# A transformer block on one core: which side work runs beside the attention, and when its banks come back

## The chip, the core and the metric

The kernel runs on one core of a Trainium2 chip. The metric is device time in microseconds (us) of one execution. Five engines work side by side: TensorE (PE in the profile) multiplies matrices into the eight banks of PSUM, VectorE (DVE) and ScalarE (ACT) read those banks, GpSimd (POOL) works in SBUF, and SyncE (SP) issues the DMAs. Each takes its own instructions in order and waits for the others by semaphores.

## The reference

One block over 2048 rows of 512 numbers, with 32 heads of width 16 that share one key and one value head, and a bilinear gated feed-forward of inner width 1792. Six vectors from a condition `c` scale, shift and gate:

```python
sa, ca, ga, sb, cb, gb = (mod[:, 0], ..., mod[:, 5])          # mod = silu(c) @ w_mod
h = _layernorm(x) * (1 + ca) + sa
q = (h @ wq) per head; k = h @ wk; v = h @ wv                  # one k and one v for all heads
o = softmax(q k^T * Dh ** -0.5) v
x = x + ga * (o @ wo)
h = _layernorm(x) * (1 + cb) + sb
x = x + gb * (((h @ w_gate) * (h @ w_up)) @ w_down)
```

## The kernel before, in words

The rows are cut into 4 blocks of 512 (numbered 0 to 3), a block into 8 units of 4 heads, a unit into 32 steps: 16 tiles of 128 keys, two heads in each step. The main loop runs over 32 units and so over 1024 steps. A step issues two score matmuls (`sc`, L549) and their exponentials on ScalarE (`P`, L551), and two matmuls (`mx`, L507) with reductions on VectorE (`mpart`, L509) that find the row maxima of a step 40 steps ahead, so that the last 40 steps of the loop have none of these. Every odd step also issues the value matmuls (`pv`, L558) of the key tile before.

All else is **side work** of an earlier block, and runs in even steps, at most six pairs of half-array matmuls at a time (`BURST`): for block b its output projection (`wo_work`, L640), its second layer norm (`ln2_work`: four sets of transposes, L683, evicted by ScalarE into `hf`, L690, and split by GpSimd into two halves in 16 bits), and its feed-forward (gate and up, then `glu`, then down, L746). `duo` runs two groups of equal length at once on the two halves of the array (L440); one group takes the PSUM bank `misc`, the other the bank `spare`. One matmul of a full group becomes one pair. Groups have 12 matmuls, those of the down projection 42. A down projection has four groups, so two duos of 84 pairs.

Three score tiles in turn use the two banks `sc` and the bank `spare`, as long as no side work is under way and `spare["held"]` is zero; otherwise they alternate between the two. When a duo ends, its first group is evicted at once. The second is evicted two ticks later (a tick is a step), and in the same call the bank is given back to the scores:

```python
        def late():
            spare["held"] -= 1
            g1.post(ps[1])
```

The queue `fill` holds the side work with a gate (the step from which it may begin) and a due step. `pace` spreads what is left over the steps up to each due step, and leaves `RESERVE` ns of it, at `PAIR` ns a pair, for after the loop. At step 16 of a block's first unit the loop appends the work of the block before: output projection, the four sets of transposes ("solo"; each takes a turn of its own in an even step, 8 steps after the output projection and then every 2), and after 2 more steps the feed-forward. From the output projection's end to the feed-forward there is thus no side work. A new duo isn't begun in the last 16 steps (`LAST_TILES`).

After the loop stands the **tail**: what is left of block 2's feed-forward and all of block 3's, as full matmuls (`plain`, L465). `cover` puts numbers of them beside the last unit's softmax sums (stored, loaded as 128 rows, inverted, stored, loaded again: L579, L582, L585, L587, L591) and beside the norm.

Rows of 512 numbers of the residual stream (`x1`) live in a ring of 4 buffers from the output projection to the end of the down projection.

## Time and profile before

| | |
|---|---|
| time, median of 3 runs | 1826.44 us (1825.76 to 1830.4) |
| the profiled execution | 1827.18 us, its span 1825.4 us |
| granted TensorE clock, mean over the span | 0.989 |
| busy: TensorE, VectorE, ScalarE, GpSimd | 94%, 79%, 67%, 27% of the span |
| first exponential of the main loop, last one's end | 103.0 us, 1659.0 us |
| the tail, to the end of the span | 166 us |

A row of a timeline gives start and length in us, engine, line, operation, what it writes and reads, the count of instructions merged into it and, in brackets, how long the engine had been idle and what released it. A row of a table by windows gives the stretch, its length, the busy time and count of PE, PEld, DVE, ACT and POOL, the granted clock (1.00 is full), the DMA's share and GB/s. A matmul's busy time counts its latency too, so that busy shares of TensorE overstate its load.

### The profile page before, as it was taken

How to read it: one execution, taken by the hardware profiler on the slowest of the kernel's cores; microseconds unless marked ns; L12 is line 12 of the kernel's file. 1: busy time of each engine (PE TensorE's matmuls, PEld its weight loads, DVE VectorE, ACT ScalarE, POOL GpSimd, SP SyncE). 2: the span in 40 equal slices, each digit the busy share in tenths (PEclk: the TensorE clock that was granted, in tenths of full speed). 3: DMA queues.
4: the chain of work that ended last, by engine and by line, in shares of the span. 5: the costliest groups of instructions: out<-in, count | busy, mean ns of one | idle time of the engine just before them, and what ended most of it. 6: DMA issues, size and time to landing. Idle time of an engine off the chain costs nothing.

```text
span 1825.4 us, 32237 instructions
## 1 busy us (share of the span) xinstructions
PE 1714.7 (94%) x12643; PEld 554.1 (30%) x12643; DVE 1438.3 (79%) x2441; ACT 1217.3 (67%) x2269; POOL 488.7 (27%) x688
## 2 busy tenths in 40 slices
PE   6899999889989999999999999999989999998999
PEld 3332222222223333333223333333223323322444
DVE  7877999999998888888998888888989888911210
ACT  4567788777777767776677767676777777772110
POOL 5834453436566811010021010100011010111130
PEclk9999999999999999999999999999999999998999
DMA  5212222112221200000100000000100000001000
GB/s 189 91 69 94 60 69 61 49 44 65 82 70 55 55 15 9 5 14 17 50 9 15 9 15 9 6 14 20 46 8 15 9 15 9 11 4 39 18 1 23
DMA packets 49795, 66.58 MB, mean 36 GB/s; under 512 B 16166, under 2 KB 30314, under 8 KB 49644
## 3 DMA queue, kind: packets, MB, share of 16 engines
q1 hardware_dynamic: 48060, 64.33, 11.4%
q8 instruction: 99, 1.62, 0.4%
q14 instruction: 52, 0.43, 0.1%
q10 hardware_dynamic: 1584, 0.20, 0.1%
HBM read 51.12 MB, written 8.92 MB: 33 GB/s over the span
## 4 chain that ended last, share of the span: by engine, by line
PE 68%; DVE 17%; ACT 10%; issue 2%; DMA 2%; POOL 1%; SPq 0%; DVEq 0%; POOLq 0%; ACTq 0%
PE pv L558 22%; PE misc L440 17%; DVE mpart L509 13%; PE mx L507 10%; PE sc L549 10%; PE misc L465 8%; ACT P L551 8%; DVE gf L731 1%; DMA xbig<-in_A_x_dram 1%; ACT ev L564 1%; DVE x L640 0%; DVE x L746 0%; ACT qf L476 0%; DVE oc L591 0%; ACT q L475 0%
## 5 line engine op out<-in xcount | busy, mean ns | idle before, releaser
L509 DVE TENSOR_REDUCE mpart<-mx 128x1 f32<-128x512 f32 x2048 | 1294.2, 684 | 172.3 <-PE sc L549 136.3
L551 ACT ACTIVATE P<-sc 128x512 f32<-128x512 f32 x2048 | 1097.7, 599 | 391.6 <-PE sc L549 385.0
L549 PE MATMUL sc<-sst,kst 50*128 50x512 f16 x2048 | 630.5, 382 | 52.7 <-ACT P L551 35.3
L507 PE MATMUL mx<-kst,sst 48*128 48x512 f16 x2048 | 656.3, 383 | 22.8 <-DVE mpart L509 19.6
L558 PE MATMUL pv<-P,vst 128*32 128x512 f32 x4096 | 552.2, 612 | 0.0
L507 PEld LDWEIGHTS <-sst 48*128 48x128 f16 x2048 | 161.8, 94 | 602.7 <-issue 545.7
L732 POOL TENSOR_SCALAR glu<-gf 128x512 f16<-128x512 f32 x56 | 34.6, 618 | 556.0 <-DVE gf L731 555.9
L549 PEld LDWEIGHTS <-kst 50*128 50x128 f16 x2048 | 136.5, 94 | 107.0 <-issue 66.8
L440 PE MATMUL misc<-h2T,wg 64*128 64x512 f16 x1008 | 134.6, 375 | 7.7 <-DVE gf L731 7.7
L558 PEld LDWEIGHTS pv<-P,vst 128*32 128x32 f32 x4096 | 81.1, 108 | 186.4 <-issue 181.7
L440 PE MATMUL misc<-h2T,wu 64*128 64x512 f16 x1008 | 132.6, 375 | 0.4 <-ACT g L725 0.4
L731 DVE TENSOR_TENSOR gf<-misc,g 128x512 f32<-128x512 f32 x56 | 38.3, 686 | 102.4 <-PE misc L465 62.9
L594 POOL TENSOR_SCALAR och<-oc 128x512 f16<-128x512 f32 x15 | 9.3, 618 | 305.4 <-DVE oc L591 165.9
L440 PE MATMUL misc<-wd,glu 64*128 64x512 f16 x672 | 85.6, 375 | 1.9 <-DVE x L746 1.1
L725 ACT ACTIVATE g<-misc 128x512 f32<-128x512 f32 x56 | 34.0, 608 | 78.7 <-PE misc L465 75.5
L465 PE MATMUL misc<-wd,glu 128*128 128x512 f16 x336 | 74.0, 382 | 0.0
L440 PEld LDWEIGHTS <-wg 64*128 64x128 f16 x1008 | 50.7, 94 | 71.8 <-issue 19.4
L440 PEld LDWEIGHTS <-wu 64*128 64x128 f16 x1008 | 50.3, 94 | 60.2 <-issue 8.8
L733 POOL TENSOR_TENSOR glu<-gf,glu 128x512 f16<-128x512 f32 x56 | 64.7, 1155 | 4.7
L440 PE MATMUL misc<-h,wq 64*128 64x512 f16 x384 | 52.9, 391 | 1.6 <-ACT qf L476 1.6
L815 POOL TENSOR_TENSOR wsl<-wsl 128x448 f32<-128x448 f32 (+1 forms) x40 | 39.0, 975 | 55.9 <-DMA wsl<-in_B_w_up_dram 30.3
L817 POOL TENSOR_TENSOR kwb<-kwb,wsl 128x448 f32<-128x448 f32 (+1 forms) x40 | 47.6, 1189 | 3.1
(214 smaller groups left out, 912.8 us busy)
## 6 DMA issues: line engine op xcount, KB each, us to landing
wsl<-in_B_w_gate_dram SPq DMA_DIRECT2D x32, 224.0 KB
wsl<-in_B_w_up_dram SPq DMA_DIRECT2D x32, 224.0 KB
wsl<-in_B_w_down_dram SPq DMA_DIRECT2D x28, 256.0 KB
sst<-qd SPq DMA_DIRECT2D x186, 32.0 KB
qd<-q SPq DMA_DIRECT2D x16, 256.0 KB
oc<-ev SPq DMA_DIRECT2D x128, 32.0 KB
rr<-ri SPq DMA_DIRECT2D x16, 256.0 KB
xl<-in_A_x_dram SPq DMA_DIRECT2D x16, 256.0 KB
```

The source lines that it names most:

```text
L440: nc.tensor.matmul(p, left[64 * r:64 * r + 64], right[64 * r:64 * r + 64], start=start, stop=stop)
L465: nc.tensor.matmul(p, left, right, start=i == 0, stop=i == g.n - 1)
L507: nc.tensor.matmul(m, s[64 * a:64 * a + 48, p, t * 128:(t + 1) * 128], kst[64 * a:64 * a + 48, kc * 512:(kc + 1) * 512], start=True, stop= ...
L509: nc.vector.tensor_reduce(mparts[u][:, a, p, t, kc:kc + 1], m, axis=AX.X, op=OP.max)
L549: nc.tensor.matmul(t, kst[64 * a:64 * a + 50, kt * 128:(kt + 1) * 128], s[64 * a:64 * a + 50, p, :], start=True, stop=True)
L551: nc.scalar.activation(ptl[u, kt, p][:, a, :], t, AF.Exp)
L558: nc.tensor.matmul(pvb[u][32 * j:32 * j + 32, :], vst[:, kt, :], ptl[u, kt, p][:, a, :], start=(kt == 0), stop=(kt == KT - 1))
L731: nc.vector.tensor_tensor(gf, p, st["g", f], op=OP.mult)
L732: nc.gpsimd.tensor_scalar(st["glu"][:, 0, f, :], gf, 1.0, 0.0, op0=OP.mult, op1=OP.add)
L733: nc.gpsimd.tensor_tensor(st["glu"][:, 1, f, :], gf, st["glu"][:, 0, f, :], op=OP.subtract)
L815: nc.gpsimd.tensor_tensor(acc if i == 0 else t, t, t, op=OP.mult)
L817: nc.gpsimd.tensor_tensor(acc, acc, t, op=OP.add)
```

## The change

Six things, in one planner:

- The second duo of a block's down projection (blocks 0 and 1) is taken out of the block's own list (`carry`) and queued behind the next block's output projection, so that it runs during that block's second norm. Block 2 keeps both its duos.
- The sets of transposes leave the queue: they stand in a list `solos` with steps of their own, run in odd steps behind the value matmuls, and write one of the three `mx` banks instead of `misc` (in the tail, for block 3, still `misc`). The last entry of the list opens the gate of the feed-forward.
- In `duo` the bank is given back to the scores three ticks after the second eviction was issued, not with it.
- A duo may begin late in the loop if its first half fits (for the down projection 16 steps before the end); what isn't done when the loop ends runs as pairs ahead of the tail, and `cover` counts it.
- Output projection and carried duo are due 64 steps after they were queued (`SOON`), the rest of the feed-forward 16 instead of 12 steps into the next block (`DUE`), in the last block 4 instead of 8 steps before the end; the reserve for the tail is 31000 ns instead of 35000.
- The ring of `x1` has 6 buffers instead of 4.

```diff
-RESERVE = 35000.0
+RESERVE = 31000.0
-DUE = 12
+DUE = 16
+SOON = 64
 QDUE = 40
-LAST_TILES = 8
+LAST_DUE = -4
...
         def late():
+            g1.post(ps[1])
+            after(3, free)
+
+        def free():
             spare["held"] -= 1
-            g1.post(ps[1])
...
-                    x1 = work.tile([128, D], F32, name="x1", tag="x1", bufs=4)
+                    x1 = work.tile([128, D], F32, name="x1", tag="x1", bufs=6)
...
-                st["p"] = ps_misc()
+                st["p"] = ps_misc() if b == NB - 1 else ps_mx()
...
-            n += 4.0 if kind == "solo" else 2 * what[0].n
+            n += 0.0 if kind == "call" else 2 * what[0].n
...
     def open_gate(step):
         if not fill:
             return False
+        if fill[0][1] == "duo" and NU * NSTEP - step < 2 * -(-fill[0][2][0].n // BURST) + 2:
+            return False
...
-            if kind == "solo":
-                _, f, post = what
-                credit[0] -= 4.0
-                f()
-                if post:
-                    posts.append(post)
-                return
-            if NU * NSTEP - step < 2 * LAST_TILES:
-                fill.appendleft(([0, 0], kind, what, due))
-                return
+            if kind == "call":
+                what(step)
+                if not open_gate(step):
+                    return
+                _, kind, what, due = fill.popleft()
             begin(step, what, due)
         parts = max(1, round(cur["turn"] / max(credit[0], 1.0)))
-        burst(step, min(-(-cur["turn"] // parts), BURST))
+        n = min(-(-cur["turn"] // parts), BURST)
+        if not cur["second"]:
+            n = max(n, -(-cur["turn"] // max((NU * NSTEP - 2 - step) // 2, 1)))
+        burst(step, n)
...
                 late_max()
+                if solos and solos[0][0] <= step:
+                    _, it = solos.popleft()
+                    if isinstance(it, list):
+                        it[0] = step
+                    else:
+                        it[1]()
+                        posts.append(it[2])
...
-                due = (b + 1) * UB * NSTEP + (DUE if b < NB - 1 else -8)
+                due = (b + 1) * UB * NSTEP + (DUE if b < NB - 1 else LAST_DUE)
                 gate = [step + 4, 0]
+                soon = step + SOON
                 for two in twos(wo_work(b - 1)):
-                    fill.append((gate, "duo", two, due))
-                for gap, it in zip((TR_GAP, LN_GAP, LN_GAP, LN_GAP), ln):
-                    fill.append(([None, gap], "solo", it, due))
-                gate = [None, FFN_GAP]
-                for two in ffn_twos(b - 1):
+                    fill.append((gate, "duo", two, soon))
+                gate = [1 << 30, 0]
+
+                def turned(step, ln=ln, gate=gate):
+
+                    solos.extend((step + TR_GAP + LN_GAP * j, it) for j, it in enumerate(ln))
+                    solos.append((step + TR_GAP + LN_GAP * len(ln) + FFN_GAP - 2, gate))
+
+                fill.append(([0, 0], "call", turned, soon))
+                for two in carry:
+                    fill.append(([0, 0], "duo", two, soon))
+                work_ = ffn_twos(b - 1)
+                carry = [] if b == NB - 1 else work_[-1:]
+                for two in work_[:len(work_) - len(carry)]:
                     fill.append((gate, "duo", two, due))
...
-    if cur["gen"] is not None:
-        assert cur["second"]
-        for _ in cur["gen"]:
-            pass
     pv(u, KT - 1)
     pv_out(u)
+    left = cur["left"]
+    if cur["gen"] is not None:
+        assert cur["second"] and NU * NSTEP - cur["swapped"] > 2
+        for _ in cur["gen"]:
+            drain_posts()
...
-    cover(6000)
+    cover(6000 - 216 * left)
```

What this makes of the order, at three places. In the changed program the line numbers are 4 higher from L507 on (L507 is L511, L549 is L553, L551 is L555, L558 is L562, L683 is L687, L690 is L694), L440 is L441 and L465 is L469.

**TensorE, one set of transposes of block 1's second norm, in unit 17.** `n` is the normalised row tile, `glu` the product of gate and up, which the down projection reads. Before:

```order
L507 MATMUL mx<-kst,sst_119 128x512
L549 LDWEIGHTS kst
L549 MATMUL sc<-sst_122,kst 128x512
...
L683 MATMUL misc<-ident,n_12405 128x128
L683 MATMUL misc<-ident,n_12426 128x128
L683 MATMUL misc<-ident,n_12445 128x128
L683 MATMUL misc<-ident,n_12460 128x128
...
L558 MATMUL pv<-P,vst 32x512 x4
```

Now:

```order
L441 LDWEIGHTS glu
L441 MATMUL misc<-wd,glu 128x512
...
L553 MATMUL sc<-sst_122,kst 128x512
...
L562 MATMUL pv<-P,vst 32x512 x4
L687 MATMUL mx<-ident,n_12251 128x128
L687 MATMUL mx<-ident,n_12280 128x128
L687 MATMUL mx<-ident,n_12299 128x128
L687 MATMUL mx<-ident,n_12324 128x128
```

The set stands behind the value matmuls instead of ahead of the next ones, in an `mx` bank, and the even step before it carries four pairs of block 0's down projection.

**ScalarE, the evictions of the same norm.** Before:

```order
L690 ACTIVATE hf<-misc,hsc 128x512
L551 ACTIVATE P<-sc 128x512 x8
L690 ACTIVATE hf<-misc,hsc 128x512
L551 ACTIVATE P<-sc 128x512 x10
L564 ACTIVATE ev<-pv 128x512
L551 ACTIVATE P<-sc 128x512 x10
L725 ACTIVATE g<-misc 128x512
```

Now:

```order
L694 ACTIVATE hf<-mx,hsc 128x512
L555 ACTIVATE P<-sc 128x512 x4
L694 ACTIVATE hf<-mx,hsc 128x512
L555 ACTIVATE P<-sc 128x512 x20
L568 ACTIVATE ev<-pv 128x512
L555 ACTIVATE P<-sc 128x512 x46
L729 ACTIVATE g<-misc 128x512
```

Four exponentials (two steps) lie between two evictions instead of eight, and the first gate eviction of the feed-forward comes some 30 exponentials later.

**SP, from the loop's end.** `oc` and `rs` take the last unit's output and sums, `rc` and `rr` are the loads of the sums, `out_dram` the result. Before:

```order
L571 DMA oc<-ev 16x512 x4
L572 DMA rs_3_21493<-ev 4x512
L579 DMA rc<-rs_3_21493 128x32
L748 DMA out_dram<-x_17550 128x512
L585 DMA ri_3_21916<-rc 128x32
L587 DMA rr<-ri_3_21916 128x1x512
```

Now:

```order
L575 DMA oc<-ev 16x512 x4
L576 DMA rs_3_21509<-ev 4x512
L752 DMA out_dram<-x_17346 128x512
L583 DMA rc<-rs_3_21509 128x32
L752 DMA out_dram<-x_17381 128x512
L589 DMA ri_3_22060<-rc 128x32
L591 DMA rr<-ri_3_22060 128x1x512
```

A store of the duo that ends after the loop now stands ahead of the first load of the sums, another ahead of the store of their inverses.

More of the change, by code (lines that the diff above doesn't have):

```diff
@@ L249, in split_rows @@
     def split_rows(dst, p, scale, mscale, bias):
-        hi = work.tile([128, BT], F16, name="hi", tag="x1", bufs=4)
+        hi = work.tile([128, BT], F16, name="hi", tag="x1", bufs=6)
         nc.scalar.activation(hi, p, AF.Identity, bias=bias, scale=mscale)
@@ L793, in m2 @@
             st["md"] = md
-        gab = work.tile([128, D], F32, name="gab", tag="x1", bufs=4)
+        gab = work.tile([128, D], F32, name="gab", tag="x1", bufs=6)
         gbb = consts.tile([128, D], F32, name="gbb")
@@ L1086, in ffn_twos @@
         return order + twos(down)
+    solos = deque()
+    carry = []
     for u in range(NU):
```

## The prediction

> **What bounds the kernel now.** I read the page first (busy shares, the chain that ended last), then the timelines of single engines, because the shares hide that the program has four kinds of stretch with four prices.
>
> ```profile
> span 1825.4 us, 32237 instructions
> 251.24 24.70 DVE mpart L509 x40
> ```
>
> The chain's long pieces are VectorE's max reductions where no side work runs. A step makes two, so 40 of them are ten pairs of steps: 24.70 / 10 = 2.47 us per pair. I count in pairs of steps, since side work is issued once in two steps. With side work TensorE's order sets the pace. These rows are TensorE's side matmuls; x6 is three side pairs (a pair is two half-array matmuls), x8 four, x10 five, x12 six, and the distance between the starts of two equal rows is one pair of steps:
>
> ```profile
> 1436.06 0.81 PE L440 MATMUL misc<-h2T,wu 64*128 64x512 f16 x6
> 1438.97 0.81 PE L440 MATMUL misc<-h2T,wu 64*128 64x512 f16 x6
> 1571.04 1.03 PE L440 MATMUL misc<-h2T,wg 64*128 64x512 f16 x8
> 1573.95 1.03 PE L440 MATMUL misc<-h2T,wg 64*128 64x512 f16 x8
> 814.21 1.24 PE L440 MATMUL misc<-wd,glu 64*128 64x512 f16 x10
> 817.26 1.24 PE L440 MATMUL misc<-wd,glu 64*128 64x512 f16 x10
> 556.20 1.46 PE L440 MATMUL misc<-h2T,wg 64*128 64x512 f16 x12
> 559.47 1.46 PE L440 MATMUL misc<-h2T,wg 64*128 64x512 f16 x12
> ```
>
> So: none 2.47, three or four 2.91, five 3.05, six 3.27 us. The first pairs cost a flat 0.44 (the scores lose their third bank), the fourth is free, the fifth and sixth cost 0.14 and 0.22. Four is the cheapest load, and a gap without side work wastes it.
>
> In the last 40 steps the max work is over, and there the price is another. Rows of ScalarE's exponentials, and one of the side work:
>
> ```profile
> 1614.47 1.46 PE L440 MATMUL misc<-h2T,wg 64*128 64x512 f16 x12
> 1614.87 1.08 ACT L551 ACTIVATE P<-sc 128x512 f32<-128x512 f32 x2
> 1617.73 2.14 ACT L551 ACTIVATE P<-sc 128x512 f32<-128x512 f32 x4 [0.46 <-PE sc L549]
> 1649.59 2.15 ACT L551 ACTIVATE P<-sc 128x512 f32<-128x512 f32 x4 [0.71 <-PE sc L549]
> 1652.45 2.35 ACT L551 ACTIVATE P<-sc 128x512 f32<-128x512 f32 x4 [0.71 <-PE sc L549]
> 1656.60 1.08 ACT L551 ACTIVATE P<-sc 128x512 f32<-128x512 f32 x2 [1.80 <-PE sc L549]
> 1658.25 3.64 PE L558 MATMUL pv<-P,vst 128*32 128x512 f32 x16
> 1661.82 15.24 PE L465 MATMUL misc<-wd,glu 128*128 128x512 f16 x66
> 1696.70 124.77 PE misc L465 x578
> ```
>
> With six side pairs 1617.73 - 1614.87 = 2.86 us; with none 1652.45 - 1649.59 = 2.86 as well. Six pairs are free here, and the kernel before leaves the last 12 steps empty. After the loop every matmul stands alone on the path: 124.77 / 578 = 0.216 us each.
>
> **The change, part by part.**
>
> *(a) The tail.* In the kernel before, 720 full matmuls stand after the loop; in the changed order 636, with 36 pairs of the down projection ahead of them. A pair has the length of one full matmul (1.46 - 0.16 over six is 0.217), so 672 stand where 720 did: 48 x 0.216 = 10.4 us less. The 48 pairs are eight bursts of six in the last eight pairs of steps, at 2.86 as before: free. One thing gets worse: the load of the softmax sums is now behind an output store on SP, which waits for VectorE's eviction after the 36 pairs.
>
> ```profile
> 1667.36 0.32 SPq L579 DMA_DIRECT2D rc<-rs  x1
> 1672.59 0.23 DVE L582 TENSOR_SCALAR rc<-rc,kb 128x32 f32<-128x32 f32 x1
> 1678.60 0.69 DVE L591 TENSOR_TENSOR oc<-oc,rr 128x512 f32<-128x512 f32 x1 [5.39 <-DMA rr<-ri]
> 1699.89 0.69 DVE L693 TENSOR_TENSOR h2T<-hf,h2T 128x512 f16<-128x512 f32 x1
> ```
>
> Before, the tail's first matmul is at 1661.82, the load goes out 5.5 us later, and the sums are worked on at 10.8. Now the pairs end 36 x 0.217 = 7.8 us after the same point, eviction (0.75) and store put the load at about 9.2, and 2 us of flight put the sums at about 11.3. The rest of that chain (6.0 us from 1672.59 to 1678.60, then the same conversions) keeps its length, and the cover ahead of the output projection grows from 66 matmuls to 36 + 38 = 74, that is 1.7 us. I charge the 0.5 us by which the sums come later, since the cover did not reach before either. Behind the second norm's transposes 18 matmuls are left as cover instead of 74, 3.9 us from 1696.70 by the old times, to 1700.6. The last conversion (1699.89 + 0.69) ended at 1700.6 too, and only the tenth gate matmul needs it, 1.9 us later: nothing is charged. Sum of (a): -9.9, between -10.4 and -6.
>
> *(b) The cold end.* The last column of these rows before the DMA share is the clock that TensorE was granted:
>
> ```profile
> 1641.00:1652.00 11.00, 7.84 (x46) 1.33 (x45) 0.00 (x0) 8.58 (x16) 2.50 (x3) 1.00 0.00 0
> 1652.00:1656.00 4.00, 3.26 (x18) 0.45 (x15) 0.00 (x0) 2.28 (x4) 0.00 (x0) 0.66 0.00 0
> 1656.00:1662.00 6.00, 5.32 (x25) 0.90 (x22) 0.00 (x0) 2.22 (x5) 0.00 (x0) 0.50 0.00 0
> ```
>
> After eleven thin microseconds the clock falls to half. The step pair from 1652.45 takes 1656.60 - 1652.45 = 4.15 instead of 2.86 (1.3 lost), and the last 16 value matmuls take 3.6 instead of about 1.95 (two rows of eight at 1.06, overlapped), 1.65 lost. With six pairs in each of these step pairs TensorE is dense, as it is at 1614 (clock 1.00). I take the whole: -3.0; if the clock falls all the same, 0.
>
> [...]
>
> *(c) The mix inside the loop.* Between the first output projection (step 272) and step 984 lie 356 pairs of steps. By the two orders: before, 46 carry no side pair, 154 two to four, 42 five, 114 six; now 15, 240, 40 and 61. With the prices above, 113.6 + 448.1 + 128.1 + 372.8 = 1062.6 before and 37.1 + 698.4 + 122.0 + 199.5 = 1057.0 now: -5.7 us. That comes from the carried half of the down projection: it fills the gaps of blocks 1 and 2, and the other bursts fall from six to four. A lower bound is no gain at all, if gaps are paid for by waits.
>
> *(d) The second bank.* When a side pair of groups ended with nothing behind it, the next scores took its bank before it was evicted:
>
> ```profile
> 925.32 1.06 PE L558 MATMUL pv<-P,vst 128*32 128x512 f32 x8
> 928.48 0.39 PE L549 MATMUL sc<-sst,kst 50*128 50x512 f16 x2 [1.77 <-DVE x L640]
> 930.41 1.93 PE L558 MATMUL pv<-P,vst 128*32 128x512 f32 x8
> 930.00:934.00 4.00, 3.87 (x22) 0.71 (x22) 2.75 (x6) 2.34 (x6) 2.02 (x9) 0.62 0.00 0
> L549 PE MATMUL sc<-sst,kst 50*128 50x512 f16 x2048 | 630.5, 382 | 52.7 <-ACT P L551 35.3 <-DVE x L640 3.9 <-ACT qf L476 1.9
> 1289.23 0.39 PE L549 MATMUL sc<-sst,kst 50*128 50x512 f16 x2 [0.98 <-DVE x L746]
> ```
>
> The waits are 3.9 + 1.9 + 1.0 = 6.8 us, and the clock falls behind them (0.62 here, the value matmuls 1.93 instead of 1.06): I put 1.2 on each of the three ends of an output projection, an estimate from this one. 10.4 in all goes, because the bank comes back three ticks later, or the carried pair follows at once. What comes instead: scores on two banks for some three steps at four places (0.44 each, 1.8), and two new borders, output projection to carried pair, priced as the border inside an output projection:
>
> ```profile
> 909.64 1.08 ACT L551 ACTIVATE P<-sc 128x512 f32<-128x512 f32 x2 [0.74 <-PE sc L549]
> 914.60 1.08 ACT L551 ACTIVATE P<-sc 128x512 f32<-128x512 f32 x2 [0.48 <-PE sc L549]
> ```
>
> 914.60 - 909.64 = 4.96, which is 1.7 over 3.27; two of them 3.4. Net -5.3, between -9 and 0.
>
> *(e) The second norm.* Its four sets of transposes leave the side bank for one of the three max banks, and move from an even step to an odd one, behind the value matmuls. ScalarE takes its evictions in order, ahead of the next exponentials:
>
> ```profile
> L690 ACT ACTIVATE hf<-misc,hsc 128x512 f32<-128x512 f32 x16 | 12.7, 798 | 2.6 <-PE misc L683 1.7 <-DVE h2T L693 0.9
> 1694.79 1.91 PE L683 MATMUL misc<-ident,n 128*128 128x128 f32 x16
> 544.11 1.08 ACT L551 ACTIVATE P<-sc 128x512 f32<-128x512 f32 x2 [0.40 <-PE sc L549]
> 548.15 1.08 ACT L551 ACTIVATE P<-sc 128x512 f32<-128x512 f32 x2 [1.32 <-PE sc L549]
> 1361.02 1.09 ACT L551 ACTIVATE P<-sc 128x512 f32<-128x512 f32 x2 [2.18 <-PE sc L549]
> 1378.02 1.08 ACT L551 ACTIVATE P<-sc 128x512 f32<-128x512 f32 x2 [0.77 <-PE sc L549]
> ```
>
> A set costs TensorE 1.91 / 4 = 0.48. The loop through it is now: eviction 0.8 plus hand-over 0.2, two exponentials 1.1, scores into their bank 0.3, value matmuls 0.95, transposes 0.48: 3.8 us against 2.91, so 0.9 for each of 12 sets, 10.8. Before, where a set met the closing of the row maxima, the pair of steps took 548.15 - 544.11 = 4.04, 1.57 over its base, and that comes once in a block: 4.7. The three last sets of block 2's norm lie in six pairs of steps that take 1378.02 - 1361.02 = 17.0, 2.2 over 6 x 2.47, 0.7 a set with a cold clock in it; for the nine sets without the maxima I take a quarter us each, 2.3, an estimate. That is 7.0 before, and net +3.8; below, -4 if the evictions find ScalarE idle; above, +8, if a set costs 1.57 everywhere and little went before.
>
> The table numbers (reserve, due times, the six buffers instead of four) act only through the order counted here; the extra buffers hold the two carried rows, and no row waits for them now.
>
> **The sum.** -9.9 - 3.0 - 5.7 - 5.3 + 3.8 = -20.1. The profiled execution took 1827.2 us for its span of 1825.4, 0.7 above the median of the runs shown; 1827.2 - 20.1 = 1807.1, or 1806.4 from the median, and I say **1806**.
>
> **Rivals.**
>
> *The inside gives back what it won.* TensorE's new borders, the two-bank scores and the norm's loop eat (c) and (d): only (a) and (b) stay, 1827.2 - 12.9 = 1814. For it: both terms rest on what the other engines do at a border, which (d) shows to vary. Against it: the prices at equal loads repeat to 0.01 us. Chance 0.16.
>
> *The norm is covered.* Transposes and evictions fall into the 0.44 us that VectorE waits anyway, (e) is -4 instead of +3.8: 1799. For it: 0.48 is about the size of that slack. Against it: the set now stands behind the value matmuls. Chance 0.12.
>
> *Slower: the norm's transposes block the max banks.* An eviction waits on ScalarE, the next max matmul waits for that bank, VectorE runs dry and TensorE's in-order queue holds the scores behind it. The wait of 2.18 in row 1361.02 is such a stop, behind a set and the row maxima together. At 2.18 + 0.9 for each of 12 sets, 37 us stand where I put 10.8: 1833. From about 2.6 us a set (10.8 + 20.1, over 12), it decides. Against it: three banks serve two reductions per step. Chance 0.04.
>
> *The end is not free.* Six pairs in every step pair press on TensorE, 3.27 instead of 2.86 (8 x 0.41 = 3.3), and the later sums leave it idle 3 us more: 1812. For it: only single bursts of six are seen there. Chance 0.07.
>
> My own sum has 0.61, within 1801 to 1811. A measurement of this kernel tells changes over about 0.3% (5.5 us). All cases but the slower one are faster by more: faster 0.94, with 0.02 for no change from mixtures of the last two. The range, from the covered norm less 3 to the inside given back plus 4, is **1796 to 1818**.
>
> **What would show it.** (a) 672 matmul lengths from the loop's end, some 10 us shorter; (b) clock near 1.00 and value matmuls at 1.06 at the loop's end; (c) side rows of x8 every 2.91 us where x12 stood; (d) no score waiting for "DVE x" or "ACT qf"; (e) pairs of steps of 3.5 to 4 us at the twelve sets. I am wrong in kind if the steps with the carried pair take over 4 us, if reductions wait on max banks, or if the tail is not shorter.

## The result, and the profile after

The changed kernel takes **1812.95 us** (median; 1806.59 to 1815.35) where the kernel before takes 1826.1 beside it: a ratio of 0.9919, with a 95% interval of 0.9905 to 0.9933. It is faster by 13 us, not by the 20 forecast, and lies inside the range (1796 to 1818) but outside the likeliest case (1801 to 1811).

The profiled execution of the changed kernel took 1815.35 us, its span 1813.5, so 11.9 less than the span before. Cut at the points that the prediction named (the first exponential of the main loop, steps 272 and 984, the last exponential's end), in us:

| stretch | before | after | difference | forecast |
|---|---|---|---|---|
| to the first exponential | 102.95 | 105.95 | +3.0 | 0 |
| to step 272 | 379.04 | 381.38 | +2.3 | 0 |
| steps 272 to 984: (c), (d), (e) | 1118.34 | 1112.25 | -6.1 | -7.2 |
| steps 984 to 1023: step pairs of (b) | 58.62 | 60.37 | +1.75 | -1.3 |
| after the loop: (a), value matmuls of (b) | 166.42 | 153.58 | -12.8 | -11.55 |
| span | 1825.4 | 1813.5 | -11.9 | -20.05 |

So two of the three parts that the change moves did nearly what the sum said. 5.3 us were lost ahead of step 272, where TensorE's matmuls are the same and in the same order as before, and 3 more than forecast in the last 40 steps.

The end of the loop in the changed kernel, in the table by windows (length, then busy time and count of PE, PEld, DVE, ACT, POOL, then the granted clock, the DMA's share and GB/s):

```profile
span 1813.5 us, 32407 instructions
1641.00:1652.00 11.00, 11.00 (x92) 4.42 (x91) 0.00 (x0) 8.14 (x16) 0.00 (x0) 1.00 0.01 1
1652.00:1656.00 4.00, 4.00 (x39) 1.68 (x38) 0.00 (x0) 2.74 (x7) 0.00 (x0) 1.00 0.00 0
1656.00:1662.00 6.00, 6.00 (x50) 2.12 (x52) 0.00 (x0) 3.83 (x7) 0.00 (x0) 1.00 0.00 0
```

The clock is 1.00 where it was 0.66 and 0.50. The timelines of TensorE, SP and VectorE behind it:

```profile
1658.93 2.12 PE L562 MATMUL pv<-P,vst 128*32 128x512 f32 x16
1660.98 7.94 PE L441 MATMUL misc<-wd,glu 64*128 64x512 f16 x72
1670.20 0.37 SPq L583 DMA_DIRECT2D rc<-rs  x1
1670.43 8.36 PE L469 MATMUL misc<-wd,glu 128*128 128x512 f16 x38 [1.51 <-DVE x L750]
1672.09 0.24 DVE L586 TENSOR_SCALAR rc<-rc,kb 128x32 f32<-128x32 f32 x1 [1.71 <-DMA rc<-rs]
```

The 16 value matmuls take 2.12 where they took 3.64. The 36 pairs end 7.9 us after the tail's first matmul; the load of the sums goes out at 9.2 and they are worked on at 11.1 (forecast: 7.8, about 9.2, 11.3). Not foreseen was the 1.51 us for which the first full matmul waits for an eviction.

Inside the loop, side matmuls of four pairs, the scores' group with its releasers (table of groups), and ScalarE's timeline over two sets of the second norm in unit 17:

```profile
625.02 1.03 PE L441 MATMUL misc<-h2T,wu 64*128 64x512 f16 x8
627.93 1.03 PE L441 MATMUL misc<-h2T,wu 64*128 64x512 f16 x8
L553 PE MATMUL sc<-sst,kst 50*128 50x512 f16 x2048 | 635.6, 382 | 39.0 <-ACT P L555 26.0 <-ACT qf L480 0.6
937.46 0.78 ACT L694 ACTIVATE hf<-mx,hsc 128x512 f32<-128x512 f32 x1 [0.70 <-PE mx L687]
938.13 2.13 ACT L555 ACTIVATE P<-sc 128x512 f32<-128x512 f32 x4
941.28 0.78 ACT L694 ACTIVATE hf<-mx,hsc 128x512 f32<-128x512 f32 x1 [1.01 <-PE mx L687]
941.95 2.13 ACT L555 ACTIVATE P<-sc 128x512 f32<-128x512 f32 x4
945.17 0.78 ACT L694 ACTIVATE hf<-mx,hsc 128x512 f32<-128x512 f32 x1 [1.09 <-PE mx L687]
```

A pair of steps with four side pairs lasts 627.93 - 625.02 = 2.91 us. The scores wait no longer for "DVE x": 52.7 us of idle before them have become 39.0, of which 26.0 are waits for their own exponentials (35.3 before). A set with side work lasts 941.95 - 938.13 = 3.82 us, against 2.91 without a set: 0.9, as forecast. ScalarE stands idle for a microsecond before each eviction.

What the prediction had no term for shows in three pairs of windows, each a window of 3.4 us and the stretch behind it:

```profile
530.50:533.90 3.40, 2.22 (x14) 0.44 (x12) 3.40 (x8) 2.09 (x4) 1.65 (x3) 1.00 0.22 64
533.90:540.70 6.80, 6.79 (x32) 1.37 (x32) 5.52 (x11) 4.77 (x9) 5.40 (x19) 0.50 0.36 104
1281.40:1284.90 3.50, 2.63 (x16) 0.59 (x16) 3.50 (x7) 2.46 (x5) 1.78 (x2) 0.99 0.33 123
1284.90:1291.70 6.80, 6.80 (x32) 1.18 (x26) 4.36 (x8) 2.96 (x6) 0.00 (x0) 0.50 0.30 93
1598.90:1602.30 3.40, 1.74 (x16) 0.47 (x16) 2.41 (x6) 1.35 (x3) 2.31 (x4) 1.00 0.00 0
1602.30:1605.70 3.40, 3.40 (x17) 0.79 (x19) 0.21 (x1) 2.04 (x4) 1.06 (x1) 0.50 0.00 0
```

At the pauses (steps without side work) of units 9 and 24 and where the row maxima of unit 30 close, TensorE is busy for 2.22, 2.63 and 1.74 us of a window, and then runs at half clock for 3.4 or 6.8 us. VectorE and ScalarE, which depend on its order, wait with it. ScalarE's timeline there:

```profile
1282.14 1.08 ACT L555 ACTIVATE P<-sc 128x512 f32<-128x512 f32 x2 [0.45 <-PE sc L553]
1283.40 1.09 ACT L555 ACTIVATE P<-sc 128x512 f32<-128x512 f32 x2 [0.18 <-PE sc L553]
1286.78 1.09 ACT L555 ACTIVATE P<-sc 128x512 f32<-128x512 f32 x2 [2.30 <-PE sc L553]
1288.05 1.09 ACT L555 ACTIVATE P<-sc 128x512 f32<-128x512 f32 x2 [0.18 <-PE sc L553]
1290.91 1.09 ACT L555 ACTIVATE P<-sc 128x512 f32<-128x512 f32 x2 [1.77 <-PE sc L553]
```

Two step pairs without side work last 1286.78 - 1282.14 = 4.64 and 1290.91 - 1286.78 = 4.13 us, where such a pair costs 2.47. Not all of that is the clock: in a kernel with the same order here and the clock at full ("the norm's transposes ahead of the value matmuls", below) the two take 3.83 and 2.62.

### The profile page after: what moved, and what is told of

The parts are those of the page before. It is cut to its first block, busy times and chain, and to the rows that moved or that the text cites. A ratio compares the mean times of both kernels' runs of the same rounds, so it can differ in the third digit from the quotient of the medians.

```text
span 1813.5 us, 32407 instructions
## 1 busy us (share of the span) xinstructions
PE 1712.6 (94%) x12727; PEld 558.2 (31%) x12727; DVE 1436.2 (79%) x2441; ACT 1221.3 (67%) x2269; POOL 490.2 (27%) x688
## 4 chain that ended last, share of the span: by engine, by line
PE 71%; DVE 15%; ACT 10%; issue 2%; DMA 1%; SPq 1%; POOL 0%; DVEq 0%; ACTq 0%; POOLq 0%
PE pv L562 23%; PE misc L441 17%; DVE mpart L513 12%; PE mx L511 10%; PE sc L553 10%; PE misc L469 8%; ACT P L555 8%; DVE gf L735 1%; ACT ev L568 1%; DMA wmA<-in_w_mod_dram 1%; ACT hf L694 1%; DVE x L644 0%; PE misc L247 0%; PE mx L687 0%; PE sc L234 0%
## 5 line engine op out<-in xcount | busy, mean ns | idle before, releaser
L555 ACT ACTIVATE P<-sc 128x512 f32<-128x512 f32 x2048 | 1099.7, 598 | 378.2 <-PE sc L553 377.0
L511 PE MATMUL mx<-kst,sst 48*128 48x512 f16 x2048 | 665.1, 384 | 23.1 <-DVE mpart L513 18.4
L553 PE MATMUL sc<-sst,kst 50*128 50x512 f16 x2048 | 635.6, 382 | 39.0 <-ACT P L555 26.0
L562 PE MATMUL pv<-P,vst 128*32 128x512 f32 x4096 | 551.5, 611 | 0.0
L511 PEld LDWEIGHTS <-sst 48*128 48x128 f16 x2048 | 159.9, 94 | 603.1 <-issue 544.2
L553 PEld LDWEIGHTS <-kst 50*128 50x128 f16 x2048 | 137.6, 94 | 98.3 <-issue 54.3
L441 PE MATMUL misc<-h2T,wg 64*128 64x512 f16 x1008 | 137.2, 376 | 10.2 <-DVE gf L735 8.9
L441 PE MATMUL misc<-h2T,wu 64*128 64x512 f16 x1008 | 134.5, 375 | 0.4 <-ACT g L729 0.4
L562 PEld LDWEIGHTS pv<-P,vst 128*32 128x32 f32 x4096 | 81.0, 108 | 169.2 <-issue 164.6
L441 PE MATMUL misc<-wd,glu 64*128 64x512 f16 x840 | 107.5, 375 | 2.7 <-DVE x L644 1.9
L441 PEld LDWEIGHTS <-wg 64*128 64x128 f16 x1008 | 50.9, 94 | 75.3 <-issue 23.1
L441 PEld LDWEIGHTS <-wu 64*128 64x128 f16 x1008 | 50.3, 94 | 61.4 <-issue 9.3
L441 PEld LDWEIGHTS <-glu 64*128 64x128 f16 x840 | 42.6, 94 | 52.2 <-issue 6.6
L469 PE MATMUL misc<-wd,glu 128*128 128x512 f16 x252 | 55.0, 379 | 1.5 <-DVE x L750 1.5
L441 PE MATMUL misc<-h,wq 64*128 64x512 f16 x384 | 54.2, 397 | 1.6 <-ACT qf L480 1.6
```

The source lines that it names most:

```text
L441: nc.tensor.matmul(p, left[64 * r:64 * r + 64], right[64 * r:64 * r + 64], start=start, stop=stop)
L469: nc.tensor.matmul(p, left, right, start=i == 0, stop=i == g.n - 1)
L511: nc.tensor.matmul(m, s[64 * a:64 * a + 48, p, t * 128:(t + 1) * 128], kst[64 * a:64 * a + 48, kc * 512:(kc + 1) * 512], start=True, stop= ...
L553: nc.tensor.matmul(t, kst[64 * a:64 * a + 50, kt * 128:(kt + 1) * 128], s[64 * a:64 * a + 50, p, :], start=True, stop=True)
L555: nc.scalar.activation(ptl[u, kt, p][:, a, :], t, AF.Exp)
L562: nc.tensor.matmul(pvb[u][32 * j:32 * j + 32, :], vst[:, kt, :], ptl[u, kt, p][:, a, :], start=(kt == 0), stop=(kt == KT - 1))
```

## The experiments

Each time stands against the kernel before on the same chip; "the changed kernel" is the one at 1812.95 us (0.9919).

**The end alone.** The kernel before with the late begin of the last duo, the pairs ahead of the tail and the smaller reserve, and nothing else of the change:

```diff
-RESERVE = 35000.0
+RESERVE = 31000.0
+        if fill[0][1] == "duo" and NU * NSTEP - step < 2 * -(-fill[0][2][0].n // BURST) + 2:
+            return False
...
-                due = (b + 1) * UB * NSTEP + (DUE if b < NB - 1 else -8)
+                due = (b + 1) * UB * NSTEP + (DUE if b < NB - 1 else -4)
...
+    cover(6000 - 216 * left)
```

> The kernel before with only the end changed: 54 more pairs in the last steps of the loop, so 666 matmul lengths stand after it where 720 did; the loop's inside, the bank and the norm as before. By my terms (a) and (b): 54 x 0.216 = 11.7 and 3.0 for the cold end, less 0.5, so -14.2 against the kernel before (ratio 0.992). If the changed kernel's whole gain is the end (theory A: the inside nets nothing), this kernel is as fast as the changed one, ratio 0.992. If the inside gained its share too (theory B: some 5 to 7 us of the -13.2 are the inside's), it is -6 to -8, ratio 0.996, and the tail's rows are not where the time went.

Measured: 1810.2 us, ratio 0.9912 (0.9897 to 0.9927), as fast as the changed kernel. The end behaves as terms (a) and (b) say (windows and timeline of this kernel):

```profile
1652.00:1656.00 4.00, 4.00 (x37) 1.74 (x34) 0.00 (x0) 2.84 (x6) 0.00 (x0) 1.00 0.00 0
1655.34 2.18 PE L558 MATMUL pv<-P,vst 128*32 128x512 f32 x16
1657.45 6.65 PE L440 MATMUL misc<-wd,glu 64*128 64x512 f16 x60
```

That is theory A's number, but the trace doesn't bear out its reason. Steps 272 to 984 take 1116.2 us here and 1112.3 in the changed kernel, which is thus 4 us better inside. It loses these again in the first two stretches (481.8 us together here, 487.3 there), in the last 40 steps (58.4 against 60.4) and in the tail (151.7 against 153.6; six matmul lengths more, 1.3). So the next question was what those stretches have in common. The equal totals alone decide nothing.

**The bank given back at once.**

```diff
         def late():
+            spare["held"] -= 1
             g1.post(ps[1])
-            after(3, free)
```

> The changed kernel with the second bank given back at once, as before; the same side pairs in the same steps. If term (d) was sized right, the scores wait for DVE x again at the places where a pair of groups ends with nothing behind it, and the time rises against the changed kernel by what is left of such places, 2 to 4 us (ratio 0.994). If the pauses' loss is the clock and not the bank (theory A), it is within 1.5 us of the changed kernel, ratio 0.992, and in its trace the step pairs at the pauses (at 417, 534 us) are as long as there.

Measured: 1815.67 us, ratio 0.9944 (0.9928 to 0.996): 2.7 us more than the changed kernel by the medians, with intervals that just overlap, so that the total alone would not carry much. The waits are back (table of groups and timeline of TensorE):

```profile
L550 PE MATMUL sc<-sst,kst 50*128 50x512 f16 x2048 | 634.8, 381 | 48.7 <-ACT P L552 26.1 <-DVE x L641 5.3 <-DVE x L747 3.1
879.29 0.39 PE L550 MATMUL sc<-sst,kst 50*128 50x512 f16 x2 [1.58 <-DVE x L747]
920.42 0.39 PE L550 MATMUL sc<-sst,kst 50*128 50x512 f16 x2 [1.76 <-DVE x L641]
1324.27 0.37 PE L550 MATMUL sc<-sst,kst 50*128 50x512 f16 x1 [1.76 <-DVE x L641]
```

Units 16, 17 and 25, where these three stand, are 1.7, 2.7 and 2.6 us longer than in the changed kernel, and each has a window of half clock behind its wait. Two more waits stand at 528.8 and 1284.8 us, in units 9 and 24. Unit 24 is 2.9 shorter all the same: the spell of half clock that the changed kernel has there is absent in this execution, and unit 30's is too (1.4). The late return does what (d) said: it takes the waits away, and 7.0 us in three units with them.

**The norm's transposes ahead of the value matmuls.**

```diff
             if p == 1:
+                if solos and solos[0][0] <= step:
+                    ...
                 if kt == 0:
                     ...
                 else:
                     pv(u, kt - 1)
                 late_max()
-                if solos and solos[0][0] <= step:
-                    ...
```

> The changed kernel with the second norm's transposes ahead of the value matmuls of their step in place of behind them; nothing else moves. If a set costs 0.9 us because its eviction is late behind the value matmuls (the loop of 3.8 us of term (e): take 0.95 - 0.48 or more out of it), each of 12 sets falls by 0.5 to 0.9, in all 6 to 9 us faster than the changed kernel, ratio 0.988. If the loss is the max bank that a set holds (rival), the order in the step does not matter: no change, ratio 0.992.

Measured: 1804.28 us, ratio 0.988 (0.9863 to 0.9898), which is the number of the first of the two theories. Its steps say something else (ScalarE's timeline over the same sets as above, then TensorE's):

```profile
934.15 0.78 ACT L694 ACTIVATE hf<-mx,hsc 128x512 f32<-128x512 f32 x1
935.31 1.08 ACT L555 ACTIVATE P<-sc 128x512 f32<-128x512 f32 x2 [0.38 <-PE sc L553]
937.59 0.78 ACT L694 ACTIVATE hf<-mx,hsc 128x512 f32<-128x512 f32 x1
938.81 1.09 ACT L555 ACTIVATE P<-sc 128x512 f32<-128x512 f32 x2 [0.44 <-PE sc L553]
936.77 0.66 PE L687 MATMUL mx<-ident,n 128*128 128x128 f32 x4
937.36 1.06 PE L562 MATMUL pv<-P,vst 128*32 128x512 f32 x8
```

The eviction no longer waits, and a set lasts 938.81 - 935.31 = 3.50 in place of 3.82: 0.33 saved on each of the eight sets beside the carried duo, less than the 0.5 to 0.9 expected. What is left over 2.91, 0.59, is what four transposes take in TensorE's order, 937.36 - 936.77. The four in unit 9, which have no side pairs beside them, stay 0.7 to 1.0 over 2.47. Together 2.7 us. The rest of the 9.4 us between the two spans goes with the clock: the spells at 1285 and 1602 us are absent (units 24 and 30 are 2.8 and 1.4 us shorter, with the same instructions in the same order), and the first exponential comes 2.0 us earlier.

**No carried half.**

```diff
-                carry = [] if b == NB - 1 else work_[-1:]
+                carry = []
```

> The changed kernel without the carried half: the down projection is done whole in its own block, and the second norm's steps have no side pairs. Prices at equal loads say +3.2 (1060.1 against 1056.9 for the 356 step pairs), the two new borders go (-3.4), and the sets of the norm lie in the open again: 12 times a price not known from this trace between 0.25 and 0.9, -7.8 to 0. By term (c) as forecast (the carried half gains): slower than the changed kernel by 0 to 3 us; if the inside gives back what the mix wins (theory A), it is as fast or faster by up to 5, ratio 0.989 to 0.992.

Measured: 1818.06 us, ratio 0.9951 (0.9934 to 0.9968): 5 us slower than the changed kernel, more than either theory had. Steps 272 to 984 take 1121.9 against 1112.3. The mix accounts for 3.0 of that. The twelve sets cost 11.3 us over their base in the open and 11.5 beside the duo, so the duo makes them no dearer. The other 6.6 stand at the pauses: nine empty step pairs are back behind the output projection in each of units 17 and 25 (four of them with a set), and there are spells of half clock at 895 (3.4 us), 936 and 1349 (6.8 each). The empty step pairs without a set stand 17.0 us over their price, against 10.2 in the changed kernel. The clock is the smaller part of that. Between the two points it is at half for 17.1 us against 13.7 in the changed kernel, and in unit 9 of this execution, where it does not fall, the four empty step pairs behind the output projection take 3.2 us more than four times 2.47 as well (in units 17 and 25, with their spells, 4.4 and 4.9 more). The carried duo is worth more than its prices, because such a pause is dear in itself, and dearer where the clock falls.

**More work in the steps without side work.** In these steps the first max matmul is issued twice into its bank:

```diff
-        nc.tensor.matmul(m, s[64 * a:64 * a + 48, p, t * 128:(t + 1) * 128],
-                         kst[64 * a:64 * a + 48, kc * 512:(kc + 1) * 512], start=True, stop=True)
+        for _ in range(2 if a == 0 and spare["thin"] else 1):
+            nc.tensor.matmul(m, ...)
```

> The changed kernel with useless work added: in steps without side work one of the step's two max matmuls is issued twice into the same bank (500 extra matmuls of 0.2 us; the output is the same). In the profiled execution of the changed kernel the clock is at half in six spells of 3.4 us in or just behind steps without side work, about 1.4 us each. Theory C (the clock): with TensorE fuller there the spells go, and the kernel with more work is faster by 4 to 9 us, ratio 0.988 to 0.990. Theory D (waits for banks and evictions, the low clock beside the point): the added matmuls cost nothing or up to 5 us, ratio 0.992 to 0.995.

Measured: 1827.31 us, ratio 1.001 (0.9999 to 1.0022), worse than both. The clock looks as theory C said: of the changed kernel's spells in the loop none is left (one, at 896 us, is new), and units 24 and 9 take 51.13 and 51.96 us in place of 53.91 and 53.00. That the added work did this in these two units is not shown: one added matmul stands in unit 24, in unit 9 they begin behind the first empty step pair, and unit 24 takes 51.13 us in the kernel with the transposes first too, which has no added work. The price was mis-set. ScalarE's timeline in a pause:

```profile
432.31 2.06 ACT L556 ACTIVATE P<-sc 128x512 f32<-128x512 f32 x4 [0.62 <-PE mx L512]
434.99 2.06 ACT L556 ACTIVATE P<-sc 128x512 f32<-128x512 f32 x4 [0.62 <-PE mx L512]
437.67 2.06 ACT L556 ACTIVATE P<-sc 128x512 f32<-128x512 f32 x4
```

A pair of steps takes 2.68 instead of 2.47: the added matmuls stand ahead of the scores in TensorE's order. (The 500 instructions of the expectation are 250 matmuls with their weight loads, 125 pairs; 125 x 0.21 = 26 us.)

**The due time 4 steps later.**

```diff
-DUE = 16
+DUE = 20
```

> The changed kernel with the due time of a block's work 4 steps later, so that the down projection lasts until the next output projection begins: the two pauses of two step pairs in blocks 2 and 3 (881 and 1282 us in the profile of the changed kernel) are gone. They took 1.39 and 2.18 + 1.66 + 0.47 over their base of 2.47, of which the base with side work (2.91) takes back 0.44 each; the other loads shift a little (+1.8 by the prices). Theory C: -3 to -5, ratio 0.989 to 0.990. If those extras are chance that falls elsewhere when it does not fall there: within 1.5 us of the changed kernel, ratio 0.992.

Measured: 1810.86 us, ratio 0.9917 (0.9903 to 0.9932): 2 us faster than the changed kernel, less than expected and not told apart from no change by the intervals. In the trace the two pauses are gone, unit 24's with its spell (units 16 and 24: 49.8 and 50.2 us in place of 50.4 and 53.9; unit 16 had no spell), and half of it is paid back in units 10 to 23, as the prices had it; steps 272 to 984 take 1110.0.

**The same useless work in the kernel before, and all three edits together.** The edits are those above.

> The kernel before with the same useless matmuls in its steps without side work (it has more of these, and six spells of half clock in them). Theory C: they go, 6 x 1.4 = 8 us, ratio 0.995 to 0.997. Theory D: no change or slower, ratio 1.000 to 1.003.

> The changed kernel with three edits at once: the second norm's transposes ahead of the value matmuls, the due time 4 steps later, and the useless matmuls in what steps without side work remain. If the three save what they should each (2.8 by the eight shorter sets, 4 by the pauses, 3 to 5 by the clock), 1800 to 1803, ratio 0.986; if the first and the third save the same spells of low clock, 1804, ratio 0.988.

Measured: 1853.51 us (1.0149; 1.0135 to 1.0164) and 1826.21 us (0.9999; 0.9988 to 1.0009). Both pay 0.21 us for every pair of empty steps, and so missed all that was expected. The kernel before even has a spell of 13.7 us at 947, in unit 17, in its profile; why a fuller kernel falls there longer was not found out. The second, which has the fewest pauses, has one spell of half clock ahead of the tail (at 66 us) and none in the loop.

**A little work at the pauses alone.** The doubled max matmul in the six steps behind the last side pair before a pause, 22 matmuls in units 1, 9, 16 and 24:

```diff
+            if cur["gen"] is not None:
+                spare["last"] = step
+            g0 = [f[0][0] for f in list(fill)[:2] if f[1] == "duo"]
+            spare["thin"] = cur["gen"] is None and 0 < step - spare["last"] <= 6 and not (
+                g0 and g0[0] is not None and g0[0] <= step)
```

> The changed kernel with the useless second max matmul only in the six steps behind the last side pair of a pause: 22 extra matmuls at four places, in place of 500. Each can cost up to 0.11 us (0.21 per step pair of two, as measured with 500), 2.4 us in all. If the losses at the pauses come with the fall of the clock (theory C), the spells of half clock at 179, 534 and 1285 us are gone, with 1.5 + 1.0 + 2.8 us of step time that went when 500 matmuls kept the clock up: net -3 against the changed kernel, between -1 and -6, ratio 0.990. If the fall of the clock only goes with a wait that stays (theory D), +2, ratio 0.993.

Measured: 1807.78 us, ratio 0.9897 (0.988 to 0.9914), 5 us less than the changed kernel, with intervals that overlap from 0.9905 to 0.9914. The windows at units 9 and 24:

```profile
528.90:532.30 3.40, 2.74 (x18) 0.67 (x18) 3.40 (x7) 1.85 (x4) 2.96 (x5) 1.00 0.02 5
532.30:539.10 6.80, 5.70 (x41) 1.50 (x41) 6.48 (x12) 6.62 (x13) 5.48 (x19) 1.00 0.45 130
1279.90:1283.30 3.40, 3.07 (x21) 0.80 (x19) 3.20 (x7) 1.92 (x5) 0.12 (x1) 1.00 0.70 233
1283.30:1290.10 6.80, 6.80 (x59) 2.15 (x56) 5.57 (x9) 4.66 (x9) 0.00 (x0) 1.00 0.00 0
```

TensorE is busy for 2.74 and 3.07 of the window instead of 2.22 and 2.63, the clock stays, and the units take 51.93 and 51.35 us instead of 53.00 and 53.91. That the work did it is not shown for unit 24: the kernel with the bank at once, the one with the transposes first and the last one below have the same pause without added work. None has a spell there, and the unit takes 50.97, 51.13 and 51.13 us. At unit 9 it is likelier: five profiles have this order and no work added at the first empty step pair, and four of them have a spell; of the three with this work (two are of kernels below) none has. In unit 1 two of these three still have it, at 178.05 and 176.84 us. The spells at 179, 418 and 1602 are gone as well; at the latter two no work was added. Nor does the total hold up: the same work added to the kernel with the transposes first, and to that with the later due time, makes neither faster (1807.68 against 1804.28 and 1806.7 against 1805.62 us). So theory C is not decided by this experiment; what a fall of the clock costs is shown better by stretches in which nothing was changed (unit 0, below).

**Combined.** The transposes first, together with this work; the same with the last block's due time one step later; and the last without any useless work:

```diff
-LAST_DUE = -4
+LAST_DUE = -3
```

> The same with the second norm's transposes ahead of the value matmuls as well. The eight shorter sets give 2.8 us whatever the clock does. Theory C: 1801 to 1805, and a smaller spread than that of the kernel with the transposes alone (1802.4 to 1808.7). If the 8.7 us of that kernel were 2.8 from the sets and the rest chance, this one is at 1807.

> The same with the last block's due time one step later (-3 in place of -4), which moves the border between an up and a gate projection from step 24 of unit 30, where the row maxima of the unit close and the changed kernel lost 2.3 us, one step pair on. If the loss comes of the two meeting, a plain border (0.5 to 0.8) is left and the half clock at 1602 us goes: 1.5 to 2 us faster than without, 1800 to 1803. If it comes of the closing alone, no change.

> The changed kernel with two edits that take work off the path and no useless matmuls: the second norm's transposes ahead of the value matmuls, and the last block's due time one step later. By the step times measured so far: 2.7 us from the eight shorter sets, 1.2 to 2.9 from the border that no longer meets the closing of the row maxima. If the median of 1804.3 of the kernel with the first edit alone came from that edit: 1801 to 1803 here. If only 2.7 of its 8.7 us did and the rest was the clock's chance: 1806 to 1809, and the spells of half clock at the pauses (near 530 and 1282 us) are there in some profiles and not in others.

Measured: 1807.68 us (0.9897; 0.9882 to 0.9911), 1806.7 us (0.9886; 0.9868 to 0.9903) and 1805.62 us (0.9878; 0.9857 to 0.9899). The first is no faster than the useless work alone, though its eight sets are 2.7 us shorter in its trace: that suggests that much of the 8.7 us of the transposes alone was the clock's chance, and the third, at 1805.6 where 1801 to 1803 or 1806 to 1809 was expected, says the same. The moved border does its part. ScalarE's timeline where unit 30's row maxima close, in the changed kernel:

```profile
1599.58 1.08 ACT L555 ACTIVATE P<-sc 128x512 f32<-128x512 f32 x2 [0.42 <-PE sc L553]
1602.31 1.08 ACT L555 ACTIVATE P<-sc 128x512 f32<-128x512 f32 x2 [1.64 <-PE sc L553]
1604.74 1.08 ACT L555 ACTIVATE P<-sc 128x512 f32<-128x512 f32 x2 [1.35 <-PE sc L553]
```

and with the border one step pair on (the second of the three kernels):

```profile
1592.97 2.17 ACT L556 ACTIVATE P<-sc 128x512 f32<-128x512 f32 x4 [0.49 <-PE sc L554]
1595.87 1.09 ACT L556 ACTIVATE P<-sc 128x512 f32<-128x512 f32 x2 [0.73 <-PE sc L554]
```

The pair of steps takes 1595.87 - 1592.97 = 2.90 in place of 5.16; 1.1 of this difference is the clock's, since the pair takes 4.07 to 4.08 in the kernels with the old border and no spell there. Since the borders of units 26 to 31 all move, these units together gain 0.9 us over those of the kernel with the useless work alone (292.2 against 293.1). The third kernel, which adds no useless work, is faster than the kernel before and than the changed one: its interval ends below that of the changed kernel.

## Why the prediction was right, and where it was wrong

**(a) Right.** 163.6 us from the tail's first matmul to the end became 152.5, that is -11.0; the forecast was -9.9. The points along the chain of the sums were met within 0.2 us. Of the rest, two things cancel that the prediction did not see. Before, TensorE waited twice for the last unit's output:

```profile
1679.81 0.39 PE L465 MATMUL misc<-wo,och 128*128 128x512 f16 x1 [0.80 <-DVE och L594]
1680.53 8.38 PE L465 MATMUL misc<-wo,och 128*128 128x512 f16 x38 [0.34 <-DVE och L595]
```

Counted from start to start these waits cost 1.5 us, and they are gone, where the prediction charged 0.5 for the later sums; the new wait for an eviction costs 1.6. That they are equal is luck. The 48 matmul lengths are 10.4 as forecast, and 0.8 belongs to (b): the first 66 matmuls of the tail no longer begin at half clock.

**(b) Right where it looked.** The clock stays at 1.00 at the loop's end, the 16 value matmuls are 1.5 us shorter and the tail's start 0.8. The last step pairs take 2.9 to 3.0 with six side pairs in each, some 0.08 more than the 2.86 that I called free, so that unit 31 gains 0.8 and not 1.3. The rival "the end is not free" (0.41 a pair) falls.

**(c) Right.** By the measured step pairs the prices are unchanged (2.91, 3.05, 3.27), and the mix gives -5.4 for -5.7. What the prices left out is that the carried duo also removes pauses.

**(e) Right.** The twelve sets stand 11.5 us over their base (forecast 10.8), and before they stood 6.8 over it (forecast 7.0): +4.7 for +3.8. The late eviction is a third of the reason beside the duo, where a set lost 0.33 when it was issued ahead of the value matmuls; the 0.59 left is the transposes' own time on TensorE, which the prediction had at 0.48. In unit 9, without side work, the sets cost 0.7 to 1.0 in both orders, where three of the four cost 0.2 before the change: why is open. The rivals "the norm is covered" and "max banks", as priced, fall.

**(d) Right in its mechanism, short in its balance.** The waits for the bank are gone but for 0.6 us for "ACT qf" at the loop's start, which had nothing to do with the bank's return, and came back with the old return. What is left for (d) when (c) and (e) are taken from -6.1 is -5.4, for -5.3 forecast (its own terms add up to -5.2). That they agree is luck: 3.6 us of the forecast were clock, and between steps 272 and 984 both profiles are at half clock for the same 13.7 us. The remainder holds two new falls, 1.1 us in unit 9 and 2.6 in unit 24 (against the kernel with 22 more matmuls): without them (d) would have been about -9.

**The step that failed** is the one that treated the low clock as belonging to the places where I had seen it. Term (b) took 3.0 for "the cold end" and term (d) 1.2 for each of three ends of an output projection, and then the sum had no clock in it any more. There was no term for what the new order makes of the other thin stretches: the pauses of units 9 and 24 (3.7 us, which the gain of (d) hid), the closing of unit 30's maxima on a border (5.16 + 3.17 us for two step pairs of 2.86, 2.6 too long; with the clock kept up by chance they take 4.07 + 2.86, so 1.4 is the clock and 1.2 the meeting), and the 5.3 us ahead of step 272. The time at half clock hardly shrank: from 60 us to the end of the span it is 37.5 us in the profile after and 39.0 before. Behind step 984 it fell from 11.7 to 3.4, as (b) said, but ahead of step 272 it rose from 13.7 to 20.5.

The 5.3 us are for the most part not an effect of the change, as far as the traces show: up to step 272 TensorE's 2919 matmuls, and all instructions of VectorE, ScalarE and GpSimd, stand in the same order before and after. (Only the later return of the bank acts there too: the first step pair behind the last duo of unit 1 takes 2.95 us in the two profiles of the changed order without a spell and without added work there, in place of 2.46.) In the fourteen profiles of this study the time of the first exponential follows the time at which the clock is first recorded at full, 14.9 to 18.5 us after the start. Six of them:

```
clock first at full   first exponential   kernel
14.9                  102.95              before
15.6                  103.38              the end alone
16.0                  103.98              transposes first
17.0                  104.68              a little work at the pauses
17.8                  105.34              bank at once
18.5                  105.95              the changed kernel
```

And unit 0, with the same instructions, takes 55.34 us in the two profiles that have no window of half clock in it, 56.4 to 56.6 in the five that have one, and 57.96 to 57.98 in the seven that have two: 1.1 to 1.3 us for one window and 2.6 for two, and nothing else differs there that the traces show. The three profiles with the old start lie between 14.9 and 15.6 and the other eleven between 16.0 and 18.5. By chance alone three of fourteen would be the lowest once in 364 times, so a part of the later start may belong to the change: the first burst of matmuls begins at 12.3 to 12.6 us in those three and at 12.6 to 12.9 in the others. Where the rest comes from was not shown.

Among the six executions of the changed kernel the one with the highest clock (0.995, the others 0.989 to 0.991) took 1806.59 us, which is the forecast: the sum was that of an execution in which the clock falls seldom. But like must be set against like: the kernel before has an execution at 0.994, of 1823.68 us, so that the change is worth some 16 to 17 us at such a clock and not 20. Over 127 executions on record, each taken against the mean of its own kernel in its group of runs, a mean granted clock lower by 0.001 goes with a span longer by 1.2 us (correlation -0.90).

The rival "the inside gives back what it won", with 1814 us and 0.16, came nearest to the time, but its mechanism did not happen: the inside kept 6.1 of its 7.2 us. The upper end of the range was taken from this rival, so that it is in part luck that the time lies inside.

## What to carry to other kernels

When a sum is made of prices read off a trace, take the granted clock as a term of its own: list the stretches that the change makes thin, by the busy time of TensorE in windows of some 3.4 us (the length of most spells here), and allow for a fall at some of them. In the profiles before and after, TensorE was busy for 1.27 to 2.54 of the 3.41 us ahead of a spell in mid-program, other stretches as thin were followed by none (below), and a fall cost 1.1 to 1.3 us for one window in unit 0 and up to 2.8 for the two windows of unit 24. A few tenths of a per cent between two executions can lie in units that the change never touches, so cut both traces at fixed points of the program before explaining a total; an experiment whose total agrees with a theory (the end alone, the transposes first, a little work at the pauses) may agree for another reason. And work that fills a thin stretch can be worth more than its prices, while work that stands ahead of others in an engine's order was not free here (0.21 us a step pair).

## What the runs showed of the hardware

**Half clock comes in spells.** In the changed kernel those behind 60 us begin at 66.30, 107.25, 178.93, 417.87, 533.92, 1284.85 and 1602.29 us. The third, the fourth and the last are 3.41 us long, the other four 6.83. In the kernel before they begin at 66.09, 103.63, 322.08, 410.83, 523.47, 929.66, 1342.67, 1359.74 and 1653.28 us; the last of these is 10.24 us long, the others 3.41. (One more begins at 1823.95, behind TensorE's last matmul.) The longest spell of the experiments is the one of 13.7 us in the kernel before with the useless work.

**TensorE is thinly busy ahead of them.** In the 3.41 us ahead of each of these spells it is busy for 1.76 to 2.54 us in the changed kernel, and for 1.27 to 2.41 us in the kernel before (without the one at 1823.95). The longest idle time between two of its matmuls behind 60 us is 1.66 us in the changed kernel and 1.77 us in the kernel before. But such a stretch is not always followed by a spell: in the changed kernel TensorE is busy for 2.26 us of the window 510.03 to 513.44, for 2.26 of 919.63 to 923.04 and for 1.91 of 1667.15 to 1670.56, in the kernel before for 2.13 of 1288.06 to 1291.47, and the clock is 1.00 in the 3.41 us behind each. What decides between the two was not shown.

**At the start the clock is first recorded at full** at 14.89 us in the kernel before and at 18.51 us in the changed one. In the 3.41 us ahead of that TensorE is busy for 2.56 and 2.92 us.

**The same pause costs more or less from one run to another**: that of unit 24 makes the unit 53.91 us long in the changed kernel, where a spell of 6.83 us follows it, and 51.13 in the one with the transposes first, where none does.
